# Single-bank score tiles, split maxima, and another step order in an attention + soft-MoE kernel

## The chip, the cores and the metric

One core of a Trainium2 chip runs the kernel. The metric is the device time of one execution in microseconds (us); three runs of the kernel before gave 554.92, 556.49 and 557.08 us, and 556.49 us is their median.

## The reference

Attention over 4 batches of 8 heads (576 positions, 64 wide), with a causal mask and a bias from a running sum of `s`, then a soft mixture of 8 experts with 4 slots each, then a two-layer feed-forward. Cut to what matters:

```python
scores = scale * np.matmul(q, k.transpose(0, 1, 3, 2))      # 32 heads, 576 x 576
scores = np.where(causal, -1e9, scores + np.minimum(bias, 0.0))
attn = np.exp(scores - np.max(scores, axis=-1, keepdims=True))
attn = attn / (np.sum(attn, axis=-1, keepdims=True) + 1e-09)
x = np.matmul(attn, v)                                       # -> (2304, 512)
logits = x @ phi                                             # 32 slots
d = softmax over tokens of logits; c = softmax over slots of logits
slot_out = per expert: relu((d.T @ x) @ w1[e]) @ w2[e]
y = c @ slot_out
out = g(y @ w_in) @ w_out                                    # 2304 x 512
```

## The kernel before, in words

All engines run a hand-written order: each engine executes its instructions in the order in which the code issues them, and a semaphore wait holds all that stands behind it on that engine. The tile framework adds a wait wherever a tile is read after another engine wrote it, or where a buffer of a rotating pool is used again.

**Attention** (the first half of the span) goes over 16 pairs of heads. The queries of a pair are five blocks of up to 128 rows, 0 to 4. Blocks are handled in four groups (`GROUPS`, L26), called here by their blocks: (3), whose causal part is 512 keys wide; N, which is the last block of 64 rows for both heads (`None`, two halves of 288 keys); (2,0), 384 and 128 keys; and (1), 256 keys. A unit is a group of a pair; there are 64, and the loop at L588 makes one step per unit, with `LAG` 2. In step i the code issues

- on TensorE (PE) the transposes T of unit i-2 (`transp`, L303), then the scores S of unit i (`s_mm`, L252 to L262);
- on VectorE (DVE) the masked maxima of unit i (`masked_min` in `softmax`, L267), in place on the scores in PSUM, each followed by the read of its accumulator;
- on ScalarE (ACT) the copies of the transposes of unit i-2 to SBUF (`evac_p`, L318 and L328), then the exponentials of unit i (`exps`, L287 and L294);
- a slice of the conversion of `w_in` (DVE L570, L572, POOL L569) and what `fill` holds for the step: loads on the SyncE queue (SP), and the parts of the slot softmax after every fourth pair (`gate_parts`, placed by `GATE_AT`).

At the end of the step in which (1) of a pair is transposed, PE gets XL of the pair before (`x_and_logits`: transposes of its output at L361 and L362, logits at L367) and then PV of this pair (`pv`: the value products, L336 for the last block, L339 for blocks 0 to 3, and ACT's copies of the result, L342 and L343). DVE then scales XL's results (`scale`, L385 to L398) and takes the reciprocals of the sums (L349 to L353).

On PE a pair therefore reads T(3), S(2,0), T(N), S(1), T(2,0), S(3) of the next pair, T(1), S(N), XL, PV.

PSUM is one pool of four buffers of two banks (`banks`, L146). The maxima of a pair are columns of one tile `nm`, and the probabilities of a group are one tile `P` for both heads.

**After attention** come the last slot softmax, the experts (L649, L665, with their weights loaded through the SP queue at L110 into SBUF, part of which attention's pools hold until they close) and the feed-forward.

Of the kernel before, what the change touches and what calls it, by code (L numbers as in the profile page):

```python
# [8 lines left out]
F32 = mybir.dt.float32  # L9
# [12 lines left out]
BIG = 1.0e30  # L22
# [3 lines left out]
GROUPS = (((3, 0),), None, ((2, 0), (0, 384)), ((1, 0),))  # L26
# [23 lines left out]
GATE_AT = dict(c0=1, d1=1, c1=2, d2=2, d3=3, d4=3, c2=3, d5=4, d6=4, c3=5)  # L50
# [3 lines left out]
def attention_softmoe_ffn_kernel(  # L54
# [82 lines left out]
    with att:  # L137
        pool = lambda n, b, **k: att.enter_context(tc.tile_pool(name=n, bufs=b, **k))
        dram = pool("dram", 1, space=bass.MemoryType.DRAM)
        ps = pool("ps", 4, space=PSUM)  # L140
        ld = pool("ld", 2)
        stage = pool("stage", 3)
        pp = pool("pp", 2)
        fx = pool("fx", 1)

        def banks():  # L146

            return ps.tile([128, 2, 512], F32, tag="s", name="s")
# [76 lines left out]
        pts_p = pool("pts", 2)  # L225
# [16 lines left out]
        s_t, P_t, nm_t, sum_t, tp_t, pts_t, r_t, ot_t = {}, {}, {}, {}, {}, {}, {}, {}  # L242

        def s_mm(pi, g):

            x, e = x_t[pi], ext[pi % 2]
            o = s_t[pi, g] = banks()
            for t, off in GROUPS[g] or ():
                n = 128 * (t + 1)
                for h, r in enumerate(halves):  # L250
                    c = 128 * t + 64 * h
                    T.matmul(out=o[:, h, off:off + n], lhsT=x[r, 0, c:c + 128], rhs=x[r, 1, 0:n], start=True, stop=False)  # L252
                for h, r in enumerate(halves):
                    T.matmul(out=o[:, h, off:off + n], lhsT=e[r, 0, 128 * t:128 * t + 128], rhs=e[r, 1, 0:n],
                             start=False, stop=True)
            for hb in range(0 if GROUPS[g] else 2):
                c = slice(288 * hb, 288 * hb + 288)
                for h, r in enumerate(halves):
                    T.matmul(out=o[r, hb, 0:288], lhsT=x[r, 0, 512 - 512 * h:576 - 512 * h], rhs=x[r, 1, c],
                             start=True, stop=False)  # L260
                for h, r in enumerate(halves):
                    T.matmul(out=o[r, hb, 0:288], lhsT=e[r, 0, 512:S], rhs=e[r, 1, c], start=False, stop=True)  # L262
# [6 lines left out]

        def softmax(pi, g):  # L270
            if pi not in nm_t:
                nm_t[pi] = small.tile([128, 12], F32, tag="nm", name="nm")
                sum_t[pi] = small.tile([128, 12], F32, tag="sum", name="sum")
            nm, o = nm_t[pi], s_t[pi, g]
            if GROUPS[g] is None:
                masked_min(o[:, 0, 0:288], tri[:, 0:288], BIG, nm[:, 9:10])
                masked_min(o[:, 1, 0:288], tri2, nm[:, 9:10], nm[:, 8:9])
            for t, off in GROUPS[g] or ():
                for h in range(2):
                    k = 2 * t + h  # L280
                    masked_min(o[:, h, off:off + 128 * (t + 1)], tri, BIG, nm[:, k:k + 1])

        def exps(pi, g):
            nm, sm, o = nm_t[pi], sum_t[pi], s_t.pop((pi, g))
            if GROUPS[g] is None:
                for hb in range(2):
                    A.activation(out=P4[:, 288 * hb:288 * hb + 288], in_=o[:, hb, 0:288], func=AF.Exp, bias=nm[:, 8:9],  # L287
                                 scale=-1.0, accum_out=sm[:, 9 + hb:10 + hb])
                return
            P = P_t[pi, g] = pp.tile([128, 2, 512], F32, tag="P", name="P")  # L290
            for t, off in GROUPS[g]:
                for h in range(2):
                    k, c = 2 * t + h, slice(off, off + 128 * (t + 1))
                    A.activation(out=P[:, h, c], in_=o[:, h, c], func=AF.Exp, bias=nm[:, k:k + 1], scale=-1.0,  # L294
                                 accum_out=sm[:, k:k + 1])

        def transp(pi, g):

            o = tp_t[pi, g] = banks()

            def both(P, c):
                for f, r in enumerate(halves):
                    T.transpose(out=o[:, f, c:c + 64], in_=P[r], identity=ident[r, r])  # L303
# [6 lines left out]
            for t, off in GROUPS[g]:  # L310
                for h in range(2):
                    for j in range(t + 1):
                        both(P[:, h, off + 128 * j:off + 128 * j + 128], 256 * h + off // 2 + 64 * j)

        def evac_p(pi, g):
            o = tp_t.pop((pi, g))
            if GROUPS[g] is None:
                A.copy(out=pt4.rearrange("p j (f q) -> p j f q", f=2),  # L318
                       in_=o[:, :, 0:320].rearrange("p f (j q) -> p j f q", q=64))
                return  # L320
            for t, off in GROUPS[g]:
                for h in range(2):
                    if (pi, h) not in pts_t:
                        pts_t[pi, h] = pts_p.tile([128, 1664], F32, tag="pts", name="pts")
                    d = pts_t[pi, h][:, 128 * t:128 * t + 128]
                    d = bass.AP(tensor=d.tensor, offset=d.offset, ap=[d.ap[0], [384, t + 1], [64, 2], [1, 64]])
                    c = 256 * h + off // 2
                    A.copy(out=d, in_=o[:, :, c:c + 64 * (t + 1)].rearrange("p f (j q) -> p j f q", q=64))  # L328

        def pv(pi):  # L330

            o = banks()
            vt = v_t[pi % 2]
            for j in range(5):
                for h, r in enumerate(halves):
                    T.matmul(out=o[r, 1, 0:64], lhsT=vt[:, j, r], rhs=pt4[:, j, r], start=(j == 0), stop=(j == 4))  # L336
            for j in range(4):
                for h, r in enumerate(halves):
                    T.matmul(out=o[r, 0, 128 * j:512], lhsT=vt[:, j, r], rhs=pts_t[pi, h][:, 512 * j:384 * j + 512],  # L339
                             start=(j == 0), stop=(j == 3))  # L340
            ot = ot_t[pi] = ot_p.tile([128, S], F32, tag="ot", name="ot")
            A.copy(out=ot[:, 512:S], in_=o[:, 1, 0:64])  # L342
            A.copy(out=ot[:, 0:512], in_=o[:, 0])  # L343
# [11 lines left out]
        def x_and_logits(pi):  # L355
            b, p = divmod(pi, 4)
            ot, o = ot_t.pop(pi), banks()
            m, mb = o[:, 0].rearrange("p (t d) -> p t d", t=4), o[:, 1]
            def x():
                for t in range(4):  # L360
                    T.transpose(out=m[:, t], in_=ot[:, 128 * t:128 * t + 128], identity=ident)  # L361
                T.transpose(out=mb[0:64, 64:192], in_=ot[:, 512:S], identity=ident)  # L362

            def logits():
                for c in range(9):
                    t, hf = divmod(c, 2)
                    T.matmul(out=mb[64 * hf:64 * hf + 64, 192 + 64 * t:256 + 64 * t], lhsT=ot[:, 64 * c:64 * c + 64],  # L367
                             rhs=phibd[:, p].rearrange("p h s -> p (h s)"), start=True, stop=True)

            for f in (logits, x) if pi == NP - 1 else (x, logits):  # L370
                f()
            return m, mb
# [39 lines left out]
        def gate_parts(b):  # L412
# [6 lines left out]
            def d2():  # L419
                lt = banks()[0:32, 0, 0:128]  # L420
# [10 lines left out]
            def d3():  # L431
                bc = banks()[:, 0]
# [19 lines left out]
            def d5():  # L452
                dn = st["dn"]
                o = banks()
                st["pa"] = pa = o[:, 0]
                st["ps"] = sums = o[:, 1]
# [50 lines left out]
            def c3():  # L507
                ct = banks()[:, 0]
# [108 lines left out]
        o = banks()  # L617
        tot, sp = o[:, 1, 0:32], o[:, 0]
# [10 lines left out]
        last_c[1](banks()[:, 0, 0:64])  # L629
# [255 lines left out]
```

## Time and profile before

| | |
|---|---|
| profiled execution | 555.6 us, of which its span 553.8 us |
| median of three runs | 556.49 us |
| PE / PE weight loads | 86% / 60% of the span busy |
| DVE / ACT / POOL | 63% / 55% / 30% |
| mean granted PE clock | 0.959 |
| chain that ended last | PE 63%, DVE 16%, ACT 11% of the span |
| DMA | 71.60 MB, mean 129 GB/s |

The shares are means over stages with different limits: attention up to about 270 us, the experts to about 330 us, where DMA is busiest, and the feed-forward to the end, where PE is busy 97% of the time. Only attention is touched by the change, so its stretches are what has to be read.

### The profile page before, as it was taken

To read this page: it belongs to the slowest core of one execution; us is meant where nothing else is said; L and a number is where in the kernel's file an instruction comes from. 1 tells how busy PE (TensorE), PEld (TensorE's weight loads), DVE (VectorE), ACT (ScalarE), POOL (GpSimd) and SP (SyncE) were. 2 spreads that over 40 slices of the span, in tenths; PEclk is the share of its full clock that TensorE was granted. 3 is DMA by queue.
4 is the path that set the end of the run, shared out by engine and by line. 5 is a ranking of instruction groups with operands and counts; after the bars stand their busy time and mean duration, and the time that the engine had idled before them with its cause. 6 is when DMAs were issued, how large, how long until landed. Compare 5 with 4: busy or idle time off the path is not lost.

```text
span 553.8 us, 12141 instructions
## 1 busy us (share of the span) xinstructions
PE 476.6 (86%) x4326; PEld 333.4 (60%) x4326; DVE 349.6 (63%) x1033; ACT 305.0 (55%) x886; POOL 163.5 (30%) x232
## 2 busy tenths in 40 slices
PE   3888887788888886886779869999999999999997
PEld 0445554455535554554356537777788888888885
DVE  5546657655666667563699379999765555545552
ACT  2666666456656666452112267666665555555553
POOL 5100110111000110010000037777754454445443
PEclk9889999988979999987599999999999999999999
DMA  2765565365645555117899993000030101101011
GB/s 66 218 196 156 153 187 164 103 172 161 174 122 149 165 157 160 53 50 227 290 378 409 407 387 114 1 1 0 3 114 1 38 2 38 39 1 39 1 40 38
DMA packets 28632, 71.60 MB, mean 129 GB/s; under 512 B 4028, under 2 KB 5436, under 8 KB 28540
## 3 DMA queue, kind: packets, MB, share of 16 engines
q1 hardware_dynamic: 28572, 70.83, 39.4%
q8 instruction: 34, 0.56, 0.4%
q14 instruction: 26, 0.21, 0.1%
HBM read 65.04 MB, written 5.16 MB: 127 GB/s over the span
## 4 chain that ended last, share of the span: by engine, by line
PE 63%; DVE 16%; ACT 11%; issue 5%; DMA 3%; SPq 0%; POOL 0%; DVEq 0%; ACTq 0%
PE o L799 10%; PE o L801 10%; PE o L800 10%; ACT P L294 9%; DVE s L267 8%; PE s L339 6%; PE s L252 6%; PE s L303 4%; PE hp L777 3%; DMA wt<-in_w_dram 3%; PE s L336 2%; PE p L649 2%; PE p L665 2%; PE s L465 2%; DVE cv L131 2%
## 5 line engine op out<-in xcount | busy, mean ns | idle before, releaser
L790 POOL TENSOR_TENSOR gl<-g,gh 128x256 fp32r<-128x256 f32 x144 | 110.9, 771 | 95.3 <-PE o L801 72.9
L267 DVE CUSTOM_DVE_ANT_0 s<-s,tri 128x512 f32<-128x512 f32 (+2 forms) x144 | 71.3, 495 | 86.0 <-ACT pts L328 40.3
L780 ACT ACTIVATE w<-w,half 128x256 f32<-128x256 f32 x144 | 73.4, 510 | 87.6 <-DVE w L779 85.3
L799 PE MATMUL o<-wt,gh 128*128 128x512 f32 x288 | 113.2, 393 | 0.2
L801 PE MATMUL o<-wt,gl 128*128 128x512 f32 x288 | 112.8, 392 | 0.3
L800 PE MATMUL o<-wt,gh 128*128 128x512 f32 x288 | 112.8, 392 | 0.0
L779 DVE TENSOR_SCALAR w<-hp 128x256 f32<-128x256 f32 x144 | 60.9, 423 | 71.2 <-PE hp L777 67.4
L294 ACT ACTIVATE P<-s,nm 128x512 f32<-128x512 f32 (+3 forms) x128 | 66.4, 531 | 57.2 <-DVE nm L267 57.2
L303 PE MATMUL s<-ident,P 64*128 64x64 f32 x800 | 47.2, 241 | 32.4 <-ACT P L294 31.5
L303 PEld LDWEIGHTS s<-ident,P 64*128 64x128 f32 x800 | 36.0, 145 | 54.4 <-ACT P L294 47.2
L801 PEld LDWEIGHTS o<-wt,gl 128*128 128x128 f32 x288 | 54.1, 188 | 13.7 <-POOL gl L790 1.9
L799 PEld LDWEIGHTS o<-wt,gh 128*128 128x128 f32 x288 | 54.3, 189 | 11.9 <-ACT gh L788 0.6
L786 DVE TENSOR_TENSOR g<-hp,w 128x256 f32<-128x256 f32 x144 | 59.7, 415 | 0.5 <-ACT w L780 0.4
L252 PE MATMUL s<-x 64*128 64x512 f32 (+3 forms) x256 | 54.3, 496 | 5.0 <-DMA x<-in_qkT_dram 5.0
L800 PEld LDWEIGHTS o<-wt,gh 128*128 128x128 f32 x288 | 54.3, 189 | 6.0
L788 ACT CAST gh<-g 128x256 fp32r<-128x256 f32 x144 | 56.3, 391 | 0.5 <-DVE g L786 0.3
L777 PE MATMUL hp<-cstack,mst 96*128 96x256 f32 x144 | 42.1, 293 | 7.3 <-DVE g L786 5.5
L328 ACT COPY pts<-s 128x512 f32<-128x512 f32 (+3 forms) x128 | 46.8, 454 | 0.0
L339 PE MATMUL s<-pts,v 128*64 128x512 f32 (+3 forms) x256 | 38.1, 435 | 0.5 <-ACT pts L328 0.5
L777 PEld LDWEIGHTS hp<-cstack,mst 96*128 96x128 f32 x144 | 27.0, 188 | 19.2 <-DVE g L786 10.4
L683 POOL TENSOR_TENSOR wt<-cv,wt 128x512 fp32r<-128x512 f32 x16 | 21.6, 1348 | 53.6 <-ACT wt L681 53.6
L405 POOL TENSOR_TENSOR Lb<-Lb 128x160 f32<-128x160 f32 x8 | 4.2, 522 | 100.2 <-DVE sum L349 100.2
(142 smaller groups left out, 650.4 us busy)
## 6 DMA issues: line engine op xcount, KB each, us to landing
wt<-in_w_dram SPq DMA_DIRECT2D x64, 512.0 KB
x<-in_qkT_dram SPq DMA_DIRECT2D x32, 288.0 KB
st<-in_w_in_dram SPq DMA_DIRECT2D x32, 256.0 KB
wt<-in_w_out_dram SPq DMA_DIRECT2D x16, 512.0 KB
out_dram<-ob SPq DMA_DIRECT2D x18, 256.0 KB
v<-in_v_main_dram SPq DMA_DIRECT2D x16, 256.0 KB
v<-in_v_tail_dram SPq DMA_DIRECT2D x16, 32.0 KB
ext<-exts SPq DMA_DIRECT2D x30, 13.5 KB
```

Of the source, the lines that this page charges most:

```text
L252: T.matmul(out=o[:, h, off:off + n], lhsT=x[r, 0, c:c + 128], rhs=x[r, 1, 0:n], start=True, stop=False)
L267: V.tensor_tensor_reduce(out=sc, in0=sc, in1=mask[:, mask.shape[1] - n:], scale=-1.0 / SCALE, scalar=init, op0=ALU.add, op1=ALU.min, accum ...
L294: A.activation(out=P[:, h, c], in_=o[:, h, c], func=AF.Exp, bias=nm[:, k:k + 1], scale=-1.0, accum_out=sm[:, k:k + 1])
L303: T.transpose(out=o[:, f, c:c + 64], in_=P[r], identity=ident[r, r])
L339: T.matmul(out=o[r, 0, 128 * j:512], lhsT=vt[:, j, r], rhs=pts_t[pi, h][:, 512 * j:384 * j + 512], start=(j == 0), stop=(j == 3))
L777: T.matmul(out=hp, lhsT=mst[0:96, 128 * c:128 * c + 128], rhs=cstack[0:96, BLK * j:BLK * j + BLK], start=True, stop=True)
L779: V.tensor_scalar(w, hp, -1.0, 1.0, op0=ALU.max, op1=ALU.min)
L780: A.activation(out=w, in_=w, func=AF.Square, bias=half, scale=0.5)
L790: G.tensor_tensor(out=gl, in0=g, in1=gh.bitcast(F32), op=ALU.subtract)
L799: T.matmul(out=o_t[j][t], lhsT=gh[:, r], rhs=wh[c], start=(c == 0), stop=False)
L800: T.matmul(out=o_t[j][t], lhsT=gh[:, r], rhs=wl[c], start=False, stop=False)
L801: T.matmul(out=o_t[j][t], lhsT=gl[:, r], rhs=wh[c], start=False, stop=(c == 15))
```

## The change: the diff, and where it moves instructions

PSUM becomes eight buffers of one bank (`bank`). Each head (or half of N) has its own score tile, each maximum its own tile (`column`), and each head of a group its own `P`. `softmax` becomes a generator: the maxima of head 0 are issued, then (after the copies of unit i-2) its exponentials, then the maxima of head 1 and its exponentials. The groups' order is (3), (2,0), N, (1). XL is issued two steps after PV of the same pair, with the scaling behind it, and PV stays at the end of a pair's fourth step. The copies of transposes go by the query half `f` instead of by head, so that each reads one bank; the one copy of N becomes two. The v load is issued a step later, the slot softmax two steps earlier.

```diff
-GROUPS = (((3, 0),), None, ((2, 0), (0, 384)), ((1, 0),))
+GROUPS = (((3, 0),), ((2, 0), (0, 384)), None, ((1, 0),))
...
-        ps = pool("ps", 4, space=PSUM)
+        ps = pool("ps", 8, space=PSUM)
-        pp = pool("pp", 2)
+        pp = pool("pp", 4)
-        def banks():
-            return ps.tile([128, 2, 512], F32, tag="s", name="s")
+        def bank():
+            return ps.tile([128, 512], F32, tag="s", name="s")
...
-            o = s_t[pi, g] = banks()
+            o = s_t[pi, g] = [bank(), bank()]
...
+        def column(n):
+            return small.tile([128, 1], F32, tag=f"nm{n}", name="nm")
...
+                for h in range(2):
+                    P = pp.tile([128, 512], F32, tag="P", name="P")
+                    P_t[pi, g].append(P)
+                    for t, off in GROUPS[g]:
+                        k, c = 2 * t + h, slice(off, off + 128 * (t + 1))
+                        nm = column(k)
+                        masked_min(o[h][:, c], tri, BIG, nm)
+                        todo.append((P[:, c], o[h][:, c], nm, k))
+                    if h == 0:
+                        yield
+                        for out_, in_, nm, k in todo:
+                            A.activation(out=out_, in_=in_, func=AF.Exp, bias=nm, scale=-1.0, accum_out=sm[:, k:k + 1])
+                        todo = []
+            yield
+            for out_, in_, nm, k in todo:
+                A.activation(out=out_, in_=in_, func=AF.Exp, bias=nm, scale=-1.0, accum_out=sm[:, k:k + 1])
...
-            for t, off in GROUPS[g]:
-                for h in range(2):
+            for h in range(2):
+                for t, off in GROUPS[g]:
                     for j in range(t + 1):
...
+            for f, o in enumerate(tp_t.pop((pi, g))):
+                if GROUPS[g] is None:
+                    A.copy(out=pt4[:, :, 64 * f:64 * f + 64], in_=o[:, 0:320].rearrange("p (j q) -> p j q", q=64))
+                    continue
...
-                at(NG * (4 * b + 4) + 3 + LAG + i, parts[n])
+                at(NG * (4 * b + 4) + 3 + i, parts[n])
...
-            at(NG * pi - 1, lambda p=pi: load_v(p))
+            at(NG * pi, lambda p=pi: load_v(p))
...
-                softmax(*units[i])
+                sf = softmax(*units[i])
+                next(sf)
             if i >= LAG:
                 evac_p(*units[i - LAG])
             if i < len(units):
-                exps(*units[i])
+                for _ in sf:
+                    pass
...
             if pi >= 0 and g == NG - 1:
-                xl = x_and_logits(pi - 1) if pi else None
                 pv(pi)
-                if xl:
-                    scale(pi - 1, *xl)
                 recips(pi)
+            if pi >= 1 and g == 1:
+                scale(pi - 1, *x_and_logits(pi - 1))
```

PE, the end of a pair's loop before: XL (L361 to L367) and PV (L336, L339) stand together, between the scores of N and the transposes of (3).

```order
L361 MATMUL s<-ident,ot 128x128 x4
L362 MATMUL s<-ident,ot 64x128
L367 MATMUL s<-phibd,ot 64x64 x9
L336 MATMUL s<-pt_152,v_154 64x64 x10
L339 MATMUL s<-pts,v_154 64x512 x2
L339 MATMUL s<-pts,v_154 64x384 x2
L339 MATMUL s<-pts,v_154 64x256 x2
L339 MATMUL s<-pts,v_154 64x128 x2
L303 MATMUL s<-ident,P 128x64 x16
L252 MATMUL s<-x 128x384 x2
```

PE with the change, the same XL (now L364 to L370):

```order
L253 MATMUL s<-ext_161 128x256
L364 MATMUL s<-ident,ot 128x128 x4
L365 MATMUL s<-ident,ot 64x128
L370 MATMUL s<-phibd,ot 64x64 x9
L308 MATMUL s<-ident,P_151 128x64 x10
L251 MATMUL s<-x 128x512 x2
```

XL now stands between the scores of (1) and the transposes of N. PV comes after T(1) and S(2,0) of the next pair, so that a pair reads T(3), S(N), T(2,0), S(1), XL, T(N), S(3) of the next pair, T(1), S(2,0) of the next pair, PV.

ACT before, from the copies of (3) on: the first exponential of a group waits for DVE, and the other three of (2,0) have no wait of their own.

```order
L328 COPY pts<-s 128x4x128 [waits Activation_49]
L294 ACTIVATE P,sum<-s,nm 128x384 [waits DVE_49]
L294 ACTIVATE P,sum<-s,nm 128x384
L294 ACTIVATE P,sum<-s,nm 128x128 x2
L318 COPY pt_152<-s 128x640 [waits PE_49]
L294 ACTIVATE P,sum<-s,nm 128x256 [waits DVE_49]
L294 ACTIVATE P,sum<-s,nm 128x256
```

ACT with the change, from the copies of N to those of PV's result (L296 is head 0's exponential, L300 head 1's, L331 the copies of transposes):

```order
L323 COPY pt_152<-s 128x5x64 [waits PE_49] x2
L296 ACTIVATE P,sum<-s,nm 128x512 [waits DVE_49]
L300 ACTIVATE P,sum<-s,nm 128x512 [waits DVE_49]
L331 COPY pts<-s 128x2x2x64 [waits PE_49] x2
L296 ACTIVATE P,sum<-s,nm 128x384 [waits DVE_49,Activation_49]
L296 ACTIVATE P,sum<-s,nm 128x128
L300 ACTIVATE P,sum<-s,nm 128x384 [waits DVE_49,Activation_49]
L300 ACTIVATE P,sum<-s,nm 128x128
L345 COPY ot<-s 128x64 [waits PE_49]
L346 COPY ot<-s 128x512 [waits PE_49]
```

Each head's exponentials have a wait of their own, and the copies of (1), with which PV's main products begin, stand behind both exponentials of (3).

## Rows read from the trace of the kernel before

**Rows 1.** Waits, whole span: who waited for whom, us in total, times, longest
```profile
PE s L303 <- ACT P L294: 31.5, 26, 2.5
...
PE s L421 <- DVE mx L417: 10.2, 4, 2.6
```
**Rows 2.** Windows: stretch, its us, busy us of each engine, PEclk, DMA share, GB/s
```profile
28.71:44.08 15.37, 13.05 (x147) 8.44 (x149) 8.03 (x34) 9.81 (x34) 0.00 (x0) 0.89 0.66 193
...
71.44:85.12 13.68, 11.30 (x148) 7.07 (x145) 8.20 (x35) 9.24 (x33) 2.65 (x6) 1.00 0.64 186
85.12:103.15 18.03, 13.63 (x172) 7.68 (x169) 12.17 (x48) 10.66 (x38) 0.32 (x1) 1.00 0.55 159
...
241.31:254.96 13.65, 10.77 (x130) 7.66 (x127) 6.28 (x28) 7.47 (x27) 1.83 (x4) 0.76 0.47 151
...
272.00:330.00 58.00, 47.94 (x876) 29.24 (x874) 43.76 (x87) 17.57 (x52) 3.46 (x5) 0.97 1.01 391
```
**Rows 3.** Timeline, PE, one pair: start us, us, engine, line, tiles, [idle before <-releaser]
```profile
73.53 0.71 PE L303 MATMUL s<-ident,P 64*128 64x64 f32 x16
74.08 0.86 PE L252 MATMUL s<-x 64*128 64x384 f32 x4
...
75.22 0.48 PE L303 MATMUL s<-ident,P 64*128 64x64 f32 x10
75.53 0.65 PE L252 MATMUL s<-x 64*128 64x256 f32 x4
...
78.36 0.40 PE L303 MATMUL s<-ident,P 64*128 64x64 f32 x6 [2.07 <-ACT P L294]
...
79.73 1.08 PE L252 MATMUL s<-x 64*128 64x512 f32 x4
...
80.86 0.60 PE L303 MATMUL s<-ident,P 64*128 64x64 f32 x8
81.39 0.70 PE L259 MATMUL s<-x 64*64 64x288 f32 x4
...
82.75 0.66 PE L361 MATMUL s<-ident,ot 128*128 128x128 f32 x4
...
84.32 0.80 PE L336 MATMUL s<-pt,v 128*64 128x64 f32 x20
84.95 2.33 PE L339 MATMUL s<-pts,v 128*64 128x512 f32 x16
87.21 0.40 PE L303 MATMUL s<-ident,P 64*128 64x64 f32 x6
```
**Rows 4.** Timeline, DVE, the same pair
```profile
75.53 0.57 DVE L267 CUSTOM_DVE_ANT_0 s<-s,tri 128x384 f32<-128x384 f32 x1 [2.87 <-ACT pts L328]
...
81.18 0.70 DVE L267 CUSTOM_DVE_ANT_0 s<-s,tri 128x512 f32<-128x512 f32 x1 [2.23 <-ACT P L294]
...
81.97 0.70 DVE L267 CUSTOM_DVE_ANT_0 s<-s,tri 128x512 f32<-128x512 f32 x1
...
84.31 0.69 DVE L385 TENSOR_TENSOR X<-s,r 128x512 f32<-128x512 f32 x1
...
85.44 0.21 DVE L398 TENSOR_TENSOR Lb<-s,r 64x64 f32<-64x64 f32 x1
```
**Rows 5.** Timeline, ACT, the same pair
```profile
77.63 0.58 ACT L294 ACTIVATE P<-s,nm 128x384 f32<-128x384 f32 x1 [2.22 <-DVE nm L267]
...
79.44 0.70 ACT L318 COPY pt<-s 128x640 f32<-128x640 f32 x1
...
83.50 0.68 ACT L294 ACTIVATE P<-s,nm 128x512 f32<-128x512 f32 x1
...
84.16 0.64 ACT L328 COPY pts<-s 128x256 f32<-128x256 f32 x2
84.67 0.53 ACT L287 ACTIVATE P<-s,nm 128x288 f32<-128x288 f32 x1
```
**Rows 6.** Timeline, SP queue, the end of attention
```profile
246.10 28.53 SPq L110 DMA_DIRECT2D wt<-in_w_dram  x15
```

More of the change, by code (lines that the diff above doesn't have):

```diff
@@ L251, in s_mm @@
                     c = 128 * t + 64 * h
-                    T.matmul(out=o[:, h, off:off + n], lhsT=x[r, 0, c:c + 128], rhs=x[r, 1, 0:n], start=True, stop=False)
+                    T.matmul(out=o[h][:, off:off + n], lhsT=x[r, 0, c:c + 128], rhs=x[r, 1, 0:n], start=True, stop=False)
                 for h, r in enumerate(halves):
-                    T.matmul(out=o[:, h, off:off + n], lhsT=e[r, 0, 128 * t:128 * t + 128], rhs=e[r, 1, 0:n],
+                    T.matmul(out=o[h][:, off:off + n], lhsT=e[r, 0, 128 * t:128 * t + 128], rhs=e[r, 1, 0:n],
                              start=False, stop=True)
@@ L258, in s_mm @@
                 for h, r in enumerate(halves):
[L259 removed]
+                    T.matmul(out=o[hb][r, 0:288], lhsT=x[r, 0, 512 - 512 * h:576 - 512 * h], rhs=x[r, 1, c],
                              start=True, stop=False)
                 for h, r in enumerate(halves):
[L262 removed]
+                    T.matmul(out=o[hb][r, 0:288], lhsT=e[r, 0, 512:S], rhs=e[r, 1, c], start=False, stop=True)
         def masked_min(sc, mask, init, out):
@@ L268, in masked_min @@
                                    op0=ALU.add, op1=ALU.min, accum_out=out)
+        def column(n):
+            return small.tile([128, 1], F32, tag=f"nm{n}", name="nm")
         def softmax(pi, g):
-            if pi not in nm_t:
-                nm_t[pi] = small.tile([128, 12], F32, tag="nm", name="nm")
+            if pi not in sum_t:
                 sum_t[pi] = small.tile([128, 12], F32, tag="sum", name="sum")
-            nm, o = nm_t[pi], s_t[pi, g]
+            sm, o = sum_t[pi], s_t.pop((pi, g))
+            todo = []
@@ L275, in softmax @@
             if GROUPS[g] is None:
-                masked_min(o[:, 0, 0:288], tri[:, 0:288], BIG, nm[:, 9:10])
-                masked_min(o[:, 1, 0:288], tri2, nm[:, 9:10], nm[:, 8:9])
-            for t, off in GROUPS[g] or ():
-                for h in range(2):
[L280 to L290, printed above, removed]
-            for t, off in GROUPS[g]:
-                for h in range(2):
-                    k, c = 2 * t + h, slice(off, off + 128 * (t + 1))
-                    A.activation(out=P[:, h, c], in_=o[:, h, c], func=AF.Exp, bias=nm[:, k:k + 1], scale=-1.0,
-                                 accum_out=sm[:, k:k + 1])
+                n0, n1 = column(8), column(9)
@@ new lines, in softmax @@
+                masked_min(o[0][:, 0:288], tri[:, 0:288], BIG, n0)
+                masked_min(o[1][:, 0:288], tri2, n0, n1)
+                todo += [(P4[:, 288 * hb:288 * hb + 288], o[hb][:, 0:288], n1, 9 + hb) for hb in range(2)]
+            else:
+                P_t[pi, g] = []
+                for h in range(2):
+                    P = pp.tile([128, 512], F32, tag="P", name="P")
[9 more added lines that the diff above has]
+                            A.activation(out=out_, in_=in_, func=AF.Exp, bias=nm, scale=-1.0, accum_out=sm[:, k:k + 1])
+                        todo = []
@@ L297, in transp @@
+            yield
+            for out_, in_, nm, k in todo:
+                A.activation(out=out_, in_=in_, func=AF.Exp, bias=nm, scale=-1.0, accum_out=sm[:, k:k + 1])
         def transp(pi, g):
-            o = tp_t[pi, g] = banks()
+            o = tp_t[pi, g] = [bank(), bank()]
             def both(P, c):
                 for f, r in enumerate(halves):
-                    T.transpose(out=o[:, f, c:c + 64], in_=P[r], identity=ident[r, r])
+                    T.transpose(out=o[f][:, c:c + 64], in_=P[r], identity=ident[r, r])
@@ L309, in transp @@
             P = P_t.pop((pi, g))
-            for t, off in GROUPS[g]:
-                for h in range(2):
+            for h in range(2):
+                for t, off in GROUPS[g]:
                     for j in range(t + 1):
-                        both(P[:, h, off + 128 * j:off + 128 * j + 128], 256 * h + off // 2 + 64 * j)
+                        both(P[h][:, off + 128 * j:off + 128 * j + 128], 256 * h + off // 2 + 64 * j)
         def evac_p(pi, g):
[L316 to L328, printed above, removed]
+            for f, o in enumerate(tp_t.pop((pi, g))):
+                if GROUPS[g] is None:
+                    A.copy(out=pt4[:, :, 64 * f:64 * f + 64], in_=o[:, 0:320].rearrange("p (j q) -> p j q", q=64))
+                    continue
+                if pi not in pts_t:
+                    pts_t[pi] = pts_p.tile([128, 2, 1664], F32, tag="pts", name="pts")
+                for t, off in GROUPS[g]:
+                    d = pts_t[pi][:, 0, 128 * t + 64 * f:128 * t + 64 * f + 64]
+                    d = bass.AP(tensor=d.tensor, offset=d.offset, ap=[d.ap[0], [1664, 2], [384, t + 1], [1, 64]])
+                    i = o.rearrange("p (h c) -> p h c", h=2)[:, :, off // 2:off // 2 + 64 * (t + 1)]
+                    A.copy(out=d, in_=i.rearrange("p h (j q) -> p h j q", q=64))
         def pv(pi):
-            o = banks()
+            m, o = bank(), bank()
             vt = v_t[pi % 2]
@@ L356, in x_and_logits @@
             b, p = divmod(pi, 4)
-            ot, o = ot_t.pop(pi), banks()
-            m, mb = o[:, 0].rearrange("p (t d) -> p t d", t=4), o[:, 1]
+            ot, m, mb = ot_t.pop(pi), bank(), bank()
+            m = m.rearrange("p (t d) -> p t d", t=4)
             def x():
@@ L419, in d2 @@
             def d2():
-                lt = banks()[0:32, 0, 0:128]
+                lt = bank()[0:32, 0:128]
                 T.transpose(out=lt, in_=st["mx"], identity=ident)
@@ L431, in d3 @@
             def d3():
-                bc = banks()[:, 0]
+                bc = bank()
                 def rescale():
@@ L453, in d5 @@
                 dn = st["dn"]
-                o = banks()
-                st["pa"] = pa = o[:, 0]
-                st["ps"] = sums = o[:, 1]
+                st["pa"] = pa = bank()
+                st["ps"] = sums = bank()
                 for t in range(5):
@@ L507, in c3 @@
             def c3():
-                ct = banks()[:, 0]
+                ct = bank()
                 for t in range(4):
@@ L614, in attention_softmoe_ffn_kernel @@
             pass
-        o = banks()
-        tot, sp = o[:, 1, 0:32], o[:, 0]
+        tot, sp = bank()[:, 0:32], bank()
         T.matmul(out=tot, lhsT=s_run.to_broadcast([128, 128]), rhs=fold, start=True, stop=True)
@@ L628, in attention_softmoe_ffn_kernel @@
         last_c[0]()
-        last_c[1](banks()[:, 0, 0:64])
+        last_c[1](bank()[:, 0:64])
     w_free += slots(ctx, "post", N_POST - N_EARLY)
```

14 lines of the change are left out of this document (7 added, 7 removed).

## The prediction

> **What bounds the kernel now.** I began with the waits. PE's largest is for ACT's exponentials before the transposes L303: 31.5 us in 26 waits, of at most 2.5 us [rows 1]. Only attention has L303, so next I cut attention into windows from one pair's main value products to the next pair's [rows 2]. An undisturbed pair takes 13.68 us. PE is busy 11.30 us of it, ACT 9.24, DVE 8.20, and the DMA engines 0.64 of the time. No engine is full; PE is nearest. Then I followed PE through one such pair [rows 3]. From start to start the steps take: T(3) 0.55, S(2,0) 1.14, T(N) 0.31, S(1) 0.76, idle 2.07, T(2,0) 1.37, S(3) 1.13, T(1) 0.53, S(N) 1.36, XL 1.57, PV 0.63 for its first part and 2.26 for the main one. That is 13.68. T(2,0) has the same 16 transposes as T(3), so 0.82 of its 1.37 is waiting too. Work is 10.79 us a pair, and waiting 2.89.
>
> The wait has a simple cause. Between the end of S(2,0) and T(2,0), PE has only T(N) and S(1) to do, 1.07 us. In that time DVE must take four maxima, 75.53 to 77.63 [rows 4, 5]. ACT begins its exponentials only when the last maximum is done, because all four are columns of one tile; it idled 2.22 us until then [rows 5]. PE resumes after the first of them (0.58). About 0.3 + 2.1 + 0.7 = 3.1 us stand against 1.07: the 2.07 us. What starved DVE before it is the other half: XL and PV run in one block of 4.46 us on PE, in which no scores come; DVE idled 2.87 us [rows 4].
>
> **The change, part by part.** *Order of steps.* I set PE's work between the end of each S and its T against what the other engines need. From the end of S to the first maximum 0.32 us pass (80.86 on PE, 81.18 on DVE) [rows 3, 4]. A maximum of 512 takes 0.79 from start to start [rows 4], an exponential of 512 0.66 [rows 5], and the four of (2,0) 1.81 (77.63 to 79.44) [rows 5].
>
> - (3): need 0.32 + 2 x 0.79 + 0.66 = 2.6; PE has T(1), S(2,0) and PV, 4.56.
> - (2,0): need 0.32 + 2.1 + half of 1.81 = 3.3; PE has PV, T(3) and S(N), 4.80 instead of 1.07.
> - N: two maxima and two exponentials, each shorter than those of 512, so under 0.32 + 4 x 0.75 = 3.3, and by length about 2.4; PE has T(2,0), S(1) and XL, 2.88.
> - (1): under 2.4 for the same reason; PE has XL, T(N) and S(3), 3.01.
>
> So all of the 2.89 us can go. What is late next is PV. Its main products need the copies of (1), which on ACT stand behind both exponentials of (3). Counted from the end of XL: T(N) and S(3) end at 0.31 + 1.13 = 1.44, the first maximum starts at 1.76, the second ends at 3.34, head 1's exponential at 4.00, and the two copies at 4.51 (84.16 to 84.67) [rows 5]. PE has T(N), S(3), T(1), S(2,0) and PV's first part in the meantime, 3.74. This is a new wait of 0.8 us. DVE's scaling, which now stands ahead of the maxima of (3), takes 84.31 to 85.65, 1.34 us [rows 4]; it is done before 1.76 and costs nothing, and would cost from there on, one for one. The new pair takes 10.79 + 0.8 = 11.6 us: 2.1 less. Over 16 pairs 33.6 us. Bounds: 16 x 2.89 = 46 if the new wait is hidden, and 21 if it is 0.79 longer (below).
>
> *Split of heads and of the maxima's tiles.* No work is added on PE and DVE. Without it, ACT would start head 0 only after head 1's maximum, and the chain above would hold both exponentials behind 3.34: 0.66 to 0.79 more in each pair. For the transposes themselves it gives nothing: with eight banks in rotation T of a unit takes the banks of its own scores, so its second transpose waits for head 1 anyway.
>
> *Copies.* One copy of 640 (0.70) becomes two of 320; two of 256 took 0.64 [rows 5]. So 0 to 0.1 us more a pair on ACT, whose 9.24 of 11.6 leave room.
>
> *Loads.* v is issued one step later and waits for PV two pairs back, done long before. In SP's queue x and w follow it. At 0.64 of 13.68 the transfers need 8.8 us of each 11.6 [rows 2], so x, issued about a pair ahead, is in time. Zero, unless they collide: 0 to 1 us a pair.
>
> *Slot softmax.* Three pairs hold it inside the loop; one takes 18.03 us, 4.35 more than a plain one [rows 2]. The transpose L421 waits 10.2 us in four times for DVE's mx [rows 1]. It is issued two steps earlier with XL, and DVE has less of a backlog. Between 0 and 2.5 each; I take 1: 3 us.
>
> *Clock.* Six of the fifteen windows have a granted clock under 1.00, the first and last shown at 0.89 and 0.76, partly at the lower level of 1.2 GHz. The first is 1.69 us longer than a plain pair [rows 2], so at most 10 us in all. PE's idle stretches of 2 us stand before them, but also in plain pairs at 1.00. With none above 1 us left I take 7 back (0 to 10).
>
> **Sum.** 33.6 + 3 + 7 = 43.6 us off the profiled execution's 555.6 gives 512.0; its time is 0.9 below the median of the runs. The gain passes to the end: the experts' loads are issued from 246.10 on, as attention's SBUF comes free [rows 6], and then DMA is busy throughout [rows 2], so their stretch moves as a whole. **512 us.**
>
> **The rivals.** *The new wait is hidden* (exponentials of (3) start earlier than I let them): 46 + 3 + 7, 499.6 us. For it: ACT idles in every pair. Against: the copies' place in the order. 0.12.
>
> *The split doesn't do what it says.* Head 0's exponentials still wait for head 1's maxima, by the banks or by a late DVE: 0.79 us more a pair, 12.6, so 525 us. Against it: their own wait in ACT's order. 0.15.
>
> *PE's clock falls.* The new loop has several short waits a pair on rotating banks. If they brought every pair to what the first window shows, the nine pairs now at 1.00 would lose 1.69 each and the six gain nothing: 512 + 15 + 7 = 534 us. The trace speaks against it: plain pairs with waits of 2.07 and four smaller ones hold 1.00 [rows 2, 3]. The Trainium skill (TensorE: Matmul & The Clock Gate, "A second HAM failure mode: psum-queue depth-cycling") tells of a kernel that cycles through PSUM banks and whose short idle stretches make the clock swing between its two levels. By that rule this rival would be likelier; the rows of this kernel do not show it. 0.05.
>
> *ACT and DVE in series make it slower.* If scaling (1.34), N's copy (0.70) and (1)'s exponentials (up to 2 x 0.66) all land inside the chain from XL to PV instead of beside PE's work, its wait is 0.8 + 3.4 = 4.2, against the 2.89 that goes: 1.3 us worse in each pair, 577 us. It decides from 2.1 us more than I reckon on that chain. Against it: these three are due before S(3) ends. 0.03.
>
> *The gain is lost behind the weights*: if their loads were held by something other than attention's end, the end would stay near 555 us. Rows 6 speak against it. 0.03.
>
> **How the numbers follow.** The forecast has 0.62, the rivals the rest. Low end: 499.6 with all 10 us of clock, 497. High end: the split lost, and little of softmax or clock back: 555.6 - 21 - 3 = 531. The range 498 to 530 leaves out the last three rivals and the edges. A measurement here tells about 0.5% (2.8 us) from no change. Faster by more: 0.62 + 0.12 + 0.15 + 0.05 = 0.94; within: 0.03; slower: 0.03.
>
> **What would show it.** Right: windows of 11.4 to 11.8 us between main value products of plain pairs; the 2.07 us wait at the transposes gone; PE waiting before the main value products 0.5 to 1.1 us for ACT's copies; clock 1.00 in nearly all pairs; the expert stretch unchanged in length. Wrong: PE still waiting over 1 us before a transpose, DVE idle 2 us or more in a pair with PE waiting at the same time, PE waiting for x, or a plain pair above 12.5 us.

## The result, and the profile after

The changed kernel takes 510.47 us (median of 4 runs, 510.1 to 511.94); the kernel before took 555.7 us beside it (554.7 to 557.08). The ratio is 0.9189, with a 95% interval of 0.9159 to 0.9219. 512.0 us was forecast, in a range of 498 to 530. A few executions, of the kernel before and of experiment 4, ran in a slower state at a lower granted clock and are left out of all times and ratios.

PE's waits over the whole span (engine, line, waited for: us, times, longest), which answer to [rows 1]:

```profile
PE s L342 <- ACT pts L331: 7.8, 12, 0.7
...
PE s L424 <- DVE mx L420: 4.6, 4, 2.6
...
PE s L308 <- ACT P L296: 1.4, 2, 1.0
```

The wait of the transposes for exponentials (31.5 us before) is 1.4 us for L296, and 0.6 for L300. A new one has come, of the main value products L342 for the copies L331 (0.5 us, once, before), never longer than 0.7 us. The windows from one pair's main value products to the next, a plain pair, one with the slot softmax, the last, and then the end of attention and the experts, answer to [rows 2]:

```profile
49.27:60.88 11.61, 10.91 (x146) 7.54 (x146) 7.91 (x34) 9.30 (x33) 2.25 (x5) 1.00 0.60 171
...
72.56:88.05 15.49, 14.30 (x179) 8.10 (x175) 11.25 (x48) 10.56 (x37) 1.60 (x4) 1.00 0.67 194
...
200.51:210.15 9.64, 9.11 (x128) 5.98 (x130) 5.32 (x25) 7.80 (x28) 1.24 (x3) 1.00 0.30 99
...
226.50:284.50 58.00, 48.80 (x876) 29.38 (x874) 44.21 (x88) 17.58 (x52) 4.18 (x5) 0.93 1.01 391
```

A plain pair has gone from 13.68 to 11.6 us, and the granted clock is 1.00 in all fifteen windows. The expert stretch is as before, 45.5 us earlier: the same 876 matmuls in a window of 58 us, DMA busy throughout, at the same 391 GB/s; only the granted clock is 0.93 where it was 0.97. PE within that plain pair, which answers to [rows 3]:

```profile
51.57 0.71 PE L308 MATMUL s<-ident,P 64*128 64x64 f32 x16
52.22 0.70 PE L258 MATMUL s<-x 64*64 64x288 f32 x4
...
53.58 0.72 PE L308 MATMUL s<-ident,P 64*128 64x64 f32 x16
54.13 0.66 PE L251 MATMUL s<-x 64*128 64x256 f32 x4
...
54.83 0.66 PE L364 MATMUL s<-ident,ot 128*128 128x128 f32 x4
...
56.25 0.53 PE L308 MATMUL s<-ident,P 64*128 64x64 f32 x10
56.61 1.23 PE L251 MATMUL s<-x 64*128 64x512 f32 x4
...
59.37 0.80 PE L339 MATMUL s<-pt,v 128*64 128x64 f32 x20
60.88 1.40 PE L342 MATMUL s<-pts,v 128*64 128x512 f32 x6 [0.70 <-ACT pts L331]
```

None of the four groups of transposes has a wait any more; T(2,0) at 53.58 takes 0.55 us to the next step (54.13), where it took 1.37 [rows 3]; T(3), the same 16 transposes, takes 0.65 here. The one wait left is at 60.88. DVE and ACT ahead of it, which answer to [rows 4, 5]:

```profile
57.24 0.21 DVE L401 TENSOR_TENSOR Lb<-s,r 64x64 f32<-64x64 f32 x1
...
58.05 0.70 DVE L266 CUSTOM_DVE_ANT_0 s<-s,tri 128x512 f32<-128x512 f32 x1 [0.61 <-PE s L253]
...
58.84 0.69 ACT L296 ACTIVATE P<-s,nm 128x512 f32<-128x512 f32 x1 [0.61 <-DVE nm L266]
...
59.52 0.68 ACT L300 ACTIVATE P<-s,nm 128x512 f32<-128x512 f32 x1
...
60.19 0.64 ACT L331 COPY pts<-s 128x256 f32<-128x256 f32 x2
```

This is the chain of the prediction, one link after the other: scaling is done at 57.45, and DVE waits for the scores of (3) until 58.05; head 0's exponential follows its maximum directly, head 1's follows head 0's, then come the copies of (1), then PV.

### The profile page after: what moved, and what is told of

Its sections match the earlier page's. It is cut to its first block, busy times and chain, and to the rows that moved or that the text cites. A ratio compares the mean times of both kernels' runs of the same rounds, so it can differ in the third digit from the quotient of the medians.

```text
span 508.4 us, 12182 instructions
## 1 busy us (share of the span) xinstructions
PE 463.0 (91%) x4326; PEld 333.3 (66%) x4326; DVE 344.0 (68%) x1033; ACT 306.0 (60%) x902; POOL 163.1 (32%) x232
## 4 chain that ended last, share of the span: by engine, by line
PE 66%; DVE 11%; ACT 10%; issue 6%; DMA 4%; SPq 1%; DVEq 0%; ACTq 0%
PE o L801 11%; PE o L802 10%; PE o L803 10%; PE s L342 6%; PE s L308 4%; PE s L251 4%; PE hp L779 4%; ACT P L300 3%; PE p L651 3%; PE s L258 3%; ACT P L296 2%; DVE cv L131 2%; PE s L370 2%; DVE s L266 2%; PE p L667 2%
## 5 line engine op out<-in xcount | busy, mean ns | idle before, releaser
L266 DVE CUSTOM_DVE_ANT_0 s<-s,tri 128x512 f32<-128x512 f32 (+2 forms) x144 | 68.9, 505 | 49.7 <-PE s L261 27.1
L801 PEld LDWEIGHTS o<-wt,gh 128*128 128x128 f32 x288 | 54.4, 189 | 11.6 <-ACT gh L790 0.3
L300 ACT ACTIVATE P<-s,nm 128x512 f32<-128x512 f32 (+2 forms) x96 | 49.8, 527 | 16.1 <-DVE nm L266 16.1
L331 ACT COPY pts<-s 128x512 f32<-128x512 f32 (+3 forms) x128 | 46.7, 443 | 1.2
L296 ACT ACTIVATE P<-s,nm 128x512 f32<-128x512 f32 (+1 forms) x64 | 34.3, 542 | 20.0 <-DVE nm L266 19.5
L342 PE MATMUL s<-pts,v 128*64 128x512 f32 (+3 forms) x256 | 37.9, 438 | 7.8 <-ACT pts L331 7.8
L308 PEld LDWEIGHTS s<-ident,P 64*128 64x128 f32 x800 | 34.1, 140 | 14.9 <-issue 5.1
L308 PE MATMUL s<-ident,P 64*128 64x64 f32 x800 | 41.2, 231 | 2.4 <-ACT P L296 1.4
## 6 DMA issues: line engine op xcount, KB each, us to landing
wt<-in_w_dram SPq DMA_DIRECT2D x64, 512.0 KB
wt<-in_w_out_dram SPq DMA_DIRECT2D x16, 512.0 KB
```

The costliest lines, as they stand in the source:

```text
L266: V.tensor_tensor_reduce(out=sc, in0=sc, in1=mask[:, mask.shape[1] - n:], scale=-1.0 / SCALE, scalar=init, op0=ALU.add, op1=ALU.min, accum ...
L300: A.activation(out=out_, in_=in_, func=AF.Exp, bias=nm, scale=-1.0, accum_out=sm[:, k:k + 1])
L308: T.transpose(out=o[f][:, c:c + 64], in_=P[r], identity=ident[r, r])
L342: T.matmul(out=o[r, 128 * j:512], lhsT=vt[:, j, r], rhs=pts_t[pi][:, h, 512 * j:384 * j + 512], start=(j == 0), stop=(j == 3))
L801: T.matmul(out=o_t[j][t], lhsT=gh[:, r], rhs=wh[c], start=(c == 0), stop=False)
```

## The experiments

"Plain pair" is the time between main value products in windows without the slot softmax at clock 1.00. The kernel before ran beside the experiments and took 555 us (1 to 4 and 7) or 557 (5, 6, 8 and 9), so that runs of different experiments can be set side by side to about 0.5%.

**1. The groups' order undone.**

```diff
-GROUPS = (((3, 0),), ((2, 0), (0, 384)), None, ((1, 0),))
+GROUPS = (((3, 0),), None, ((2, 0), (0, 384)), ((1, 0),))
```

> The changed kernel with the old order of the groups, (3), N, (2,0), (1); banks, split and the later XL stay. Theory (each unit's transposes need PE work between them and the scores): between S(2,0) and T(2,0) PE has T(N) 0.31, S(1) 0.76 and XL 1.57, 2.6 us, against a need of about 3.3, so 0.7 us of wait comes back there and the wait before the main value products stays at 0.55; a plain pair takes 12.0 us and the run about 517 us. Rival (the groups' order is what made the gain): the 2.07 us wait comes back whole, 13.7 us a pair, about 543 us.

Measured: 528.78 us (524.63 to 531.24), ratio 0.9516 (0.9416 to 0.9616). A plain pair takes 12.10 us, near the 12.0 expected, with 0.64 us of wait at T(2,0) and 0.44 before the main value products. What was not expected lies in the windows with the slot softmax (columns as in [rows 2]), one with a fallen clock and one without:

```profile
75.00:96.14 21.14, 18.89 (x178) 9.85 (x174) 11.68 (x48) 10.80 (x37) 1.61 (x4) 0.76 0.50 143
...
188.66:205.38 16.72, 14.48 (x186) 8.26 (x182) 12.14 (x50) 10.86 (x38) 1.62 (x4) 1.00 0.54 153
```

In the first of them PE waits 2.02 us for the slot softmax's exponentials:

```profile
82.53 0.44 PE L462 MATMUL s<-one_t,dn 128*32 128x1 f32 x10 [2.02 <-ACT dn L453]
```

The three such windows take 21.14, 19.75 and 16.72 us where the changed kernel has 15.5, 11 us more in all, which is why the run took 12 us more than the 517 expected. So in plain pairs the groups' order is worth 0.5 us, not 2.1; the rival, at 13.7 us a pair, falls too.

**2. XL beside PV again.**

```diff
             if pi >= 0 and g == NG - 1:
+                xl = x_and_logits(pi - 1) if pi else None
                 pv(pi)
+                if xl:
+                    scale(pi - 1, *xl)
                 recips(pi)
-            if pi >= 1 and g == 1:
-                scale(pi - 1, *x_and_logits(pi - 1))
...
-                at(NG * (4 * b + 4) + 3 + i, parts[n])
+                at(NG * (4 * b + 4) + 3 + LAG + i, parts[n])
```

> The changed kernel with XL back beside PV, in one block at the end of a pair's fourth step, with the slot softmax two steps later; groups' order, banks and split stay. Theory: N has only T(2,0) and S(1), 1.31 us, of PE work before its transposes, against 2.4, so 1.1 us of wait appear there; in exchange the wait before the main value products goes, because XL's 1.57 us now cover it. A plain pair 11.9 us, the run about 515 us. Rival (the block of XL and PV starves the other engines, as it did before): most of the old 2.89 us of waits return, 13.5 us a pair, about 540 us.

Measured: 512.81 us (511.92 to 514.58), ratio 0.9255 (0.9222 to 0.9289). A plain pair takes 11.61 us, as with the change; the only wait of PE that the timeline lists in one is this:

```profile
43.95 0.89 PE L308 MATMUL s<-ident,P 64*128 64x64 f32 x10 [0.23 <-ACT P L300]
```

The wait before the main value products is gone, as expected. At N 0.23 us come instead of 1.1, and another 0.27 of idle time is spread over PE's steps (11.11 us busy of 11.61). N's need was taken too large: from the end of S(N) to the transposes 1.54 us pass (42.41 to 43.95), not 2.4. DVE begins on N's first half at 42.01, and the first transposes start before N's second exponential ends (44.28). Where XL stands makes no difference to a plain pair: DVE's longest wait in one is 1.41 us, against 2.87 before [rows 4], so the block of XL and PV no longer starves it.

**3. Two-bank tiles again.** Four tiles of two banks, and the maxima of a unit issued ahead of all its exponentials.

```diff
-        ps = pool("ps", 8, space=PSUM)
+        ps = pool("ps", 4, space=PSUM)
...
-        def bank():
-            return ps.tile([128, 512], F32, tag="s", name="s")
+        def pair():
+            o = ps.tile([128, 2, 512], F32, tag="s", name="s")
+            return [o[:, 0], o[:, 1]]
...
-            o = s_t[pi, g] = [bank(), bank()]
+            o = s_t[pi, g] = pair()
```

> The changed kernel with PSUM again as four tiles of two banks, and all maxima of a unit issued before its exponentials, so that the exponentials of head 0 wait for the last maximum of the unit; order of groups and XL stay. Theory (split worth one maximum and one exponential on the chain to the main value products): 0.66 to 0.79 us more a pair, 12.3 us, the run about 522 us. Rival (the split is worth nothing, only the order counts): 11.6 us a pair and 510 to 511 us.

Measured: 537.16 us (534.64 to 541.36), ratio 0.9698 (0.9605 to 0.9792); a plain pair takes 13.16 us:

```profile
41.34:54.50 13.16, 11.16 (x145) 7.04 (x145) 8.27 (x34) 9.42 (x32) 1.81 (x4) 1.00 0.74 201
```

Both expectations are wrong, and the theory's by twice its term. One pair, of its timeline of all engines:

```profile
45.87 0.47 DVE L270 CUSTOM_DVE_ANT_0 s<-s,tri 128x288 f32<-128x288 f32 x1 [3.56 <-PE s L265]
...
48.08 1.19 ACT L330 COPY pts<-s 128x384 f32<-128x384 f32 x4
...
49.33 1.13 PE L255 MATMUL s<-x 64*128 64x512 f32 x4 [0.47 <-ACT pts L330]
...
50.82 0.70 DVE L270 CUSTOM_DVE_ANT_0 s<-s,tri 128x512 f32<-128x512 f32 x1 [1.04 <-PE s L257]
...
51.61 0.70 DVE L270 CUSTOM_DVE_ANT_0 s<-s,tri 128x512 f32<-128x512 f32 x1
...
52.46 0.69 ACT L299 ACTIVATE P<-s,nm 128x512 f32<-128x512 f32 x1 [1.62 <-DVE nm L270]
...
54.50 0.65 PE L341 MATMUL s<-pts,v 128*64 128x512 f32 x2 [1.52 <-ACT pts L330]
```

ACT's first exponential (52.46) begins after the second maximum (51.61) is done, although each maximum has its own tile. From the first maximum of (3) to the main value products 3.68 us pass (50.82 to 54.50), against 2.83 with the change (58.05 to 60.88): that is the 0.8 us that was expected, and the wait at the end, 1.52, shows it. But S(3) also waits 0.47 us for the copies of (2,0). Experiments 5 to 7 follow this.

**4. The split alone**, on the kernel before: edits 1 and 2 together.

> The kernel before with the split alone: one-bank tiles, own tiles for each maximum, exponentials between the maxima; old order of groups and XL beside PV. Theory: T(2,0) still has 1.07 us of PE work ahead of it; head 0's exponentials can end at 2.3 us after S(2,0) and head 1's at 3.3, so the two waits at T(2,0) fall from 2.89 to about 1.9: 12.7 us a pair, the run about 540 us. Rival (order is all): 13.5 us or more a pair, 553 to 556 us. Rival (split is all): near 511 us.

Measured: 536.73 us (535.61 to 539.64), ratio 0.9694 (0.963 to 0.9757). A plain pair takes 12.4 us; six of the fifteen windows are longer at a lower clock (last section). PE's waits for head 0's exponentials add up to 11.8 us, for head 1's to 2.9:

```profile
PE s L308 <- ACT P L296: 11.8, 15, 1.0
...
PE s L308 <- ACT P L300: 2.9, 10, 0.3
```

The waits at T(2,0) fall from 2.89 us to 1.3, further than the theory had (1.9), and neither rival's time came. The four corners can be set side by side. Plain pairs: 13.68 before; 12.4 with one-bank tiles and their split alone; 13.16 with the new order of steps and two-bank tiles (experiment 3, which keeps the copies by query half and a `P` for each head); 11.60 with both. The tiles are worth 1.28 us alone and 1.56 on top of the order, the order 0.52 alone and 0.80 on top of the tiles.

**5. The maxima as columns of one tile**, which is what the prediction blamed; all of a unit's maxima issued before its exponentials; one-bank tiles kept. N's maxima stay as they are.

```diff
+                nms = small.tile([128, 8], F32, tag=f"nms{g}", name="nms")
...
-                        nm = column(k)
+                        nm = nms[:, k:k + 1]
...
-                    if h == 0:
-                        yield
-                        for out_, in_, nm, k in todo:
-                            A.activation(out=out_, in_=in_, func=AF.Exp, bias=nm, scale=-1.0, accum_out=sm[:, k:k + 1])
-                        todo = []
```

> The changed kernel with the maxima of a unit as columns of one tile and all issued before the exponentials; one-bank tiles stay. Theory after the first runs (the two-bank score tile made ACT wait for the last maximum, not the tile of the maxima): no change, 11.6 us a pair, 510 to 511 us. Rival (as the prediction had it, the maxima's tile makes ACT wait): 0.66 to 0.79 us more a pair, 521 to 523 us.

Measured: 510.59 us (510.44 to 513.16), ratio 0.9194 (0.9129 to 0.9259); a plain pair takes 11.60 us. ACT begins head 0's exponential while head 1's maximum is still running:

```profile
58.75 0.73 DVE L266 CUSTOM_DVE_ANT_0 s<-s,tri 128x512 f32<-128x512 f32 x1
...
58.93 0.69 ACT L296 ACTIVATE P<-s,nms 128x512 f32<-128x512 f32 x1 [0.60 <-DVE nms L266]
```

So neither the tile of the maxima nor the order in which maxima and exponentials are written matters. Experiment 3 issues in the same order and differs in the tiles of two banks, so these made ACT wait for the last maximum: the code writes the masked scores back into the score tile, and ACT began after the last of those writes.

**6. Head 1's exponentials first**, so that ACT begins after the last maximum although each head has its bank.

```diff
-                    if h == 0:
-                        yield
...
-                        todo = []
+                todo = todo[len(todo) // 2:] + todo[:len(todo) // 2]
```

> The changed kernel with head 1's exponentials ahead of head 0's on ACT, so that each unit's exponentials begin after its last maximum, as before the change, with everything else kept. Theory (this alone is one maximum or exponential on the chain to the main value products): 0.66 to 0.79 us more a pair, 12.3 us, 521 to 523 us; what the two-bank tiles cost beyond that (13.16 us a pair) is then the sharing of banks itself. Rival (all that the two-bank tiles cost is this wait): 13.1 us a pair, about 537 us.

Measured: 522.01 us (519.97 to 522.36), ratio 0.9376 (0.932 to 0.9432); a plain pair takes 12.25 us:

```profile
51.77:64.02 12.25, 10.90 (x145) 7.43 (x145) 7.92 (x34) 9.41 (x32) 2.25 (x5) 1.00 0.55 164
```

PE's wait before the main value products grows to this:

```profile
PE s L338 <- ACT pts L327: 16.3, 15, 1.3
```

The theory's number. The split by head is worth 0.65 us a pair; the remaining 0.91 of what two-bank tiles cost is something else.

**7. N's halves in the other order on PE**, alone and with edit 6. DVE's first maximum of N then cannot begin before both halves are done, as with a two-bank tile.

```diff
-            for hb in range(0 if GROUPS[g] else 2):
+            for hb in (1, 0) if GROUPS[g] is None else ():
```

> The changed kernel with the two halves of N's scores computed in the other order on PE, so that DVE's first maximum of N, which takes the first half, can begin only when both halves are done, as with a two-bank tile. Theory (a good part of what shared banks cost is this later start: in the two-bank run DVE begins N 0.6 us later, ACT's copies of (2,0) stand behind N's exponentials, and S(3) waits 0.47 us for them): 0.3 to 0.6 us more a plain pair, 11.9 to 12.2 us, 515 to 519 us. Rival (N has time to spare, 2.9 us of PE work against 2.4): 11.6 us and 510 to 511 us.

> The same, and head 1's exponentials first on ACT: one-bank tiles with both of the waits that two-bank tiles would bring. Theory (the two waits are what shared banks cost): 12.25 + 0.3 to 0.6 + what they add to each other, 12.6 to 13.1 us a plain pair, 527 to 536 us. Rival (shared banks cost in another way, through buffers that come free later): 12.25 us, 522 us.

Measured: alone 519.67 us (518.67 to 523.49), ratio 0.9355 (0.9298 to 0.9412), a plain pair 12.08 us; with edit 6 530.69 us (528.35 to 532.47), ratio 0.9543 (0.9479 to 0.9606), a plain pair 12.73. The plain pair of the first, then of the second:

```profile
50.91:62.99 12.08, 11.43 (x145) 7.69 (x146) 7.91 (x34) 9.30 (x33) 2.20 (x5) 1.00 0.61 171
```
```profile
40.15:52.88 12.73, 11.43 (x145) 7.54 (x146) 7.91 (x34) 9.41 (x32) 1.83 (x4) 1.00 0.73 206
```

In the first, DVE begins N late, and the second head's part of S(3) waits for ACT's copies of (2,0):

```profile
55.44 0.47 DVE L266 CUSTOM_DVE_ANT_0 s<-s,tri 128x288 f32<-128x288 f32 x1 [2.90 <-PE s L261]
...
58.88 0.18 PEld L251 LDWEIGHTS s<-x 64*128 64x128 f32 x1 [0.25 <-ACT pts L331]
```

The first maximum of N starts 4.53 us after the main value products (50.91), as with two-bank tiles (45.87 after 41.34), against 3.92 with the change. So this is 0.48 us a pair, and it adds to edit 6 (0.65) almost exactly. Together they explain 1.13 of the 1.56 us. Where the last 0.43 lies can be read from the traces. In the second run, of its timeline of all engines:

```profile
49.40 0.70 DVE L266 CUSTOM_DVE_ANT_0 s<-s,tri 128x512 f32<-128x512 f32 x1 [1.08 <-ACT pt L319]
...
50.02 0.73 DVE L266 CUSTOM_DVE_ANT_0 s<-s,tri 128x512 f32<-128x512 f32 x1
...
50.84 0.69 ACT L296 ACTIVATE P<-s,nm 128x512 f32<-128x512 f32 x1 [1.20 <-DVE nm L266]
```

Here the first maximum of (3) starts 9.25 us after the main value products (40.15), with two-bank tiles 9.48 (50.82 after 41.34): 0.23. From it to the first exponential 1.44 us pass, with two-bank tiles 1.64: 0.20. Most of this is the second maximum, which starts 0.62 us after the first on a score tile of its own and 0.79 after it on a shared one. No run tries either alone.

**8. DVE's scaling made longer**: its first product done three times.

```diff
-            V.tensor_tensor(out=xn[:, 0:4].rearrange("p t (h d) -> p t h d", h=2),
...
+            for _ in range(1 if pi == NP - 1 else 3):
+                V.tensor_tensor(out=xn[:, 0:4].rearrange("p t (h d) -> p t h d", h=2),
...
```

> The changed kernel with the first product of DVE's scaling done three times instead of once (the same result). Theory (scaling is free until the scores of (3) are there and costs one for one from then on): two more products are 1.2 us, of which 0.6 us fit into DVE's wait before the maxima of (3); 0.6 us more a plain pair, 12.2 us, about 519 us. Rival (DVE's work as such costs): 1.2 us a pair, 528 us; or it has room: 510 us.

Measured: 526.58 us (526.21 to 526.72), ratio 0.9465 (0.941 to 0.9519). DVE in a plain pair:

```profile
57.29 2.13 DVE L389 TENSOR_TENSOR X<-s,r 128x512 f32<-128x512 f32 x3
...
60.00 0.68 DVE L266 CUSTOM_DVE_ANT_0 s<-s,tri 128x512 f32<-128x512 f32 x1
```

The three products take 2.05 us to the next instruction, 1.45 more than one; 0.61 fitted into DVE's wait ahead of the maxima of (3), so 0.84 should come out, and a plain pair takes 12.36 us, 0.76 more. The rule of the prediction holds there, though the whole run came nearer to the first rival's 528 us than to the theory's 519. Eight plain pairs make 6 of the 16 us. The rest lies in the three pairs with the slot softmax and the three just before them, which were not reckoned: one takes 13.53 us (62.81 to 76.34, at a clock of 0.96) where the changed kernel has 11.68.

**9. The copies of (1) ahead of the exponentials of (3)**, the wait that the change left. As in edit 5, all of a unit's maxima are issued before its exponentials; the excerpt does not show that part.

```diff
+        late = None
...
-                for _ in sf:
-                    pass
+                if late is not None:
+                    for _ in late:
+                        pass
+                    late = None
+                if units[i][1] == 0 and i > 0:
+                    late = sf
+                else:
+                    for _ in sf:
+                        pass
```

> The changed kernel with the copies of (1) ahead of the exponentials of (3) on ACT (those are issued one step later; maxima of a unit are issued together). Theory (the 0.70 us before the main value products is ACT's queue order and nothing else): T(1) is done right after S(3), before the first maximum of (3), so the copies cost the exponentials nothing; the wait goes, a plain pair takes 10.9 us, twelve waits of 0.5 to 0.7 are saved, about 502 us. Rival (the copies only push the same 0.7 us to the next transposes or to the end of the chain): 509 to 511 us.

Measured: 502.12 us (500.64 to 503.87), ratio to the kernel before 0.9026 (0.8981 to 0.9072); beside it on the same chip edit 5, which is as fast as the changed kernel, took 510.59. A plain pair:

```profile
47.29:57.97 10.68, 10.68 (x151) 7.45 (x149) 7.91 (x34) 9.21 (x33) 2.26 (x5) 1.00 0.60 171
```

and ACT in the next of its timeline:

```profile
56.25 0.65 ACT L326 COPY pts<-s 128x256 f32<-128x256 f32 x2
56.81 0.69 ACT L295 ACTIVATE P<-s,nm 128x512 f32<-128x512 f32 x1
57.48 0.68 ACT L295 ACTIVATE P<-s,nm 128x512 f32<-128x512 f32 x1
```

The copies fill the time in which ACT had waited for the first maximum, so they cost nothing, and PE has no idle time left in a plain pair: 10.68 us busy of 10.68, 0.2 less than expected. The three pairs just before the slot softmax still take 11.6 us. This kernel beats both others.

## Why the prediction was right, and where its reasons were not

The time came out as forecast because the sum was made for all edits together, on one chain, and in part by luck: its two smaller terms were off by 1.6 us too much and up to 2.6 too little. By its terms:

- *The pair.* 13.68 to 11.60 us, 2.08 less where 2.1 was reckoned; the new wait 0.70 where 0.8 was, and PE's work 10.91 where 10.79 was. Over the fifteen windows this is 31.2 us of the 45.4 that the span lost, and the first pair gave 2.6 more; 33.6 were reckoned for sixteen. The waits of the transposes went in plain pairs, the table of PE's work against the other engines' need held, and scaling was free.
- *The share of the parts was wrong.* The prediction gave the step order the 2.1 us and the split 0.66 to 0.79 of it. In plain pairs the tiles and split are worth 1.28 alone and 1.56 on top, the order 0.52 and 0.80, the place of XL nothing. Two steps failed, and neither touched the sum, in which both edits stand together. First, "because all four are columns of one tile": it was the two-bank score tile (experiments 3 and 5). Second, a bank of its own was reckoned as useful to head 0's exponentials alone (0.65, as reckoned). It also lets DVE begin N on its first half (0.48), which the prediction did not look at; the last 0.43 is placed by the traces (experiment 7) but tried by no run.
- *Slot softmax.* The windows that hold it cost 4.35 us over a plain pair before and 3.89 now; 0.46 each, 1.4 us in all, where 3 were reckoned. L421, now L424, still waits, 4.6 us in four times.
- *Clock.* All fifteen windows are at 1.00, where six were below. From the first main value products to the last, 226.25 us became 184.08 (28.71 to 254.96, and 26.07 to 210.15), 42.2 less. Fifteen pairs at 2.08 and the softmax's 1.4 are 32.6; the other 9.6 fall on those six windows, most of it clock, where 7 was taken with 10 as bound. The stretches after attention gave 0.6.
- *The rivals.* The hidden wait (499.6 us) did not come by itself; edit 9, which hides it, gives 502. The lost split (525) is edit 6, 522. The clock's fall did not come: with a wait of 0.70 us in each plain pair and eight rotating banks the granted clock is 1.00 in all fifteen windows, so the rule of the Trainium skill named there (TensorE: Matmul & The Clock Gate, "A second HAM failure mode: psum-queue depth-cycling") is not borne out by this loop. Yet the loop of experiment 4, on the same eight banks and with waits of 1.0 and 0.3 us, still fell below 1.00 in six of fifteen windows, as many as before, so the rival was nearer than it was taken to be. The prediction argued from four smaller waits beside that of 2.07 us; the timeline of that pair lists one, of 0.17. Series and lost gain did not come either: the last main value products came 45 us sooner and the end moved by as much.

## What to carry to other kernels

Set PE's work between a result and the instruction that needs it against what the other engines do in between, unit by unit, and then ask which in-order queue the next thing stands in: that gave both the time of this change and the 8 us that it left on ACT. Here a score tile in PSUM was waited for as a whole (experiments 3 and 5), so two results that different engines take up at different times want banks of their own. When several edits hit one chain, a right sum says nothing about the shares: only undoing them one at a time does.

## What the runs showed of the hardware

The length of PE's waits did not decide whether the granted clock fell. With the split alone (experiment 4) two neighbouring pairs without the slot softmax, and a part of the second, read (columns as in [rows 2])

```profile
51.92:64.31 12.39, 11.06 (x151) 7.34 (x149) 7.79 (x35) 9.21 (x33) 1.83 (x4) 1.00 0.61 165
64.31:78.08 13.77, 12.47 (x151) 7.76 (x149) 8.09 (x36) 9.68 (x34) 2.66 (x6) 0.88 0.70 201
72.00:75.00 3.00, 3.00 (x18) 1.25 (x16) 0.88 (x3) 2.29 (x10) 0.41 (x1) 0.50 0.59 157
```

and PE's waits in them

```profile
57.95 0.63 PE L308 MATMUL s<-ident,P 64*128 64x64 f32 x8 [1.01 <-ACT P L296]
58.86 0.63 PE L308 MATMUL s<-ident,P 64*128 64x64 f32 x8 [0.28 <-ACT P L300]
70.35 0.63 PE L308 MATMUL s<-ident,P 64*128 64x64 f32 x8 [1.02 <-ACT P L296]
71.26 0.63 PE L308 MATMUL s<-ident,P 64*128 64x64 f32 x8 [0.28 <-ACT P L300]
```

After the same waits the clock stayed at 1.00 in the first pair and was 0.50, the lower of its two levels (1.2 GHz), from 72 to 75 us in the second, which took 1.38 us more. With two-bank tiles (experiment 3) waits of 1.52 us in the plain pairs left all fifteen windows at 1.00, and before the change plain pairs with a wait of 2.07 us [rows 3] were at 1.00 [rows 2]. What does decide was not tried.

Two masked maxima in a row started 0.62 us apart on score tiles of their own and 0.79 on one shared tile (experiment 7). A VectorE product done three times in a row on the same operands took 2.05 us to the next instruction (57.29 to 59.34, experiment 8), so each repeat added 0.72, where one alone takes 0.60 in the changed kernel (56.11 to 56.71). The reason for either was not tried.
